# 48-column state products, V's scalings in blocks, and a plainer end, in a delta-rule + GELU kernel

## The chip, the cores and the metric

The kernel runs on one core of one Trainium2 chip. Five engines share the work: TensorE (PE in the profile; its weight loads are the row PEld), VectorE (DVE), ScalarE (ACT), GpSimd (POOL) and SyncE (SP), which here only issues DMAs. The metric is the time of one execution on the device, in microseconds. The profile is that of one execution, and its span runs from the first to the last instruction.

## The reference

Two blocks follow each other. The first is a delta rule, a linear attention whose state is corrected at each of 768 steps, for 4 x 8 heads of 48 elements. The second is a two-layer network with an exact GELU on the 3072 tokens.

```python
k_n = k / (np.linalg.norm(k, axis=-1, keepdims=True) + 1e-06)
state = zeros((B, H, D, D))                      # B=4, H=8, S=768, D=48
for t in range(S):
    y[:, :, t] = q[:, :, t] @ state              # per head
    v_old      = state^T k_t
    state      = state + beta_t * outer(k_t, v_t - v_old)
x = y.transpose(0, 2, 1, 3).reshape(3072, 384)
h = x @ w_in                                     # 384 -> 2048
g = 0.5 * h * (1.0 + erf(h / sqrt(2)))
out = g @ w_out                                  # 2048 -> 384
```

## The kernel before

The sequence is cut into 12 chunks of 64 steps (`C = 64`, `NC = 12`). A unit is one chunk of two batches, so a chunk has two units (`u.a` is 0 or 1); the two batches lie in the two halves of the 128 partitions. `D` is 48, `H` is 8, `NP` is 4 pairs of heads, `NA` is 2. The scaled differences inside a chunk are found with a triangular inverse of 32-row blocks, which VectorE computes for two chunks at a time (`eliminate`), and 32x32 products on TensorE join the blocks (`psJ`). K in memory isn't normalised: V is multiplied by K's norm instead.

The state step of a chunk is `against_state` (old values and outputs from the state), `solve`, `outputs`, and `turn`:

```python
    HALF = [slice(0, C), slice(C, 2 * C)]
    QUADS = [(0, 0), (1, 1), (0, 1), (1, 0)]

    def scale_head(u, h):
        nc.scalar.mul(u.V[:, h], u.V[:, h], ns[u.c][:, u.a, h:h + 1])

    def scale_v(u, engine=nc.gpsimd):
        engine.tensor_tensor(u.V, u.V, ns[u.c][:, u.a].unsqueeze(2).to_broadcast([128, H, D]),
                                op=ALU.mult)
    ...
    def use(us):
        for u in us:
            psY = dn("psY")
            u.psY = quarters(psY[:, :, 0:NP * D])
            u.psS = psY[:, :, NP * D:2 * NP * D].rearrange("q p (j d) -> q p j d", d=D)
            ...                                  # u.psY: 64-column products of P and U
            if u.c > 0:
                update(u)

    def update(u):
        if u.c < NC - 1:
            for j in range(NP):
                for r, p in QUADS:
                    nc.tensor.matmul(u.psS[HALF[r], p, j, :], lhsT=u.Kp[HALF[p], 2 * j + r, :],
                                     rhs=u.U[HALF[p], 2 * j + r, :], start=True, stop=True)

    def next_state(u):
        if u.c < NC - 1:
            nc.vector.tensor_tensor(St[:, u.a], St[:, u.a], u.psS, op=ALU.add)

    def read(u, copy=nc.scalar.copy):            # x = psY + y, four operations
        ...

    def outputs(us):
        use(us)
        for u in us:
            next_state(u)
            read(u)
```

A row of K holds 48 elements and 16 columns of zeros (`Kp` is 64 wide), so the product has 64 rows per head, of which 48 count. `turn` transposes x on TensorE into `xT`, and ScalarE copies it out of PSUM. The network follows. The first layer, `fc1`, makes 128 rows of h at a time for the 256 tokens of a chunk; two PSUM buffers ("mlp") alternate, and ScalarE's GELU empties them. From chunk 2 on the second layer is a 2x2 block product with 7 products in place of 8; T1 to T4 are sums and differences of the weights. Its products use the same two "mlp" buffers, plus one for Z:

```python
    def fc1(c, f):
        psH = ps.tile([128, NA * 128], F32, tag="mlp", name="psH")
        for m in range(NM):
            nc.tensor.matmul(psH, lhsT=w_in_sb[...], rhs=xTs[c][:, m, :], ...)
        nc.scalar.activation(G[:, f, :], psH, ACT.Gelu)

    def send(u, cols=slice(0, DM), queues=(nc.scalar, nc.scalar)):
        for p in range(2):
            row = (2 * u.a + p) * S + u.c * C
            queues[p].dma_start(out=out[row:row + C, cols], in_=u.o[HALF[p], cols])

    def fc2(u, f0, f1):                          # chunks 0 and 1 only
        ...                                      # psO, an "mlp" buffer, one per unit
        if f1 == NF:
            u.o = wk.tile([128, DM], F32, tag="o_sb", name="o_sb")
            nc.scalar.copy(u.o, u.psO)
            send(u)

    def sums_of_w():
        for n, a, b in ((1, B12, B11), (2, B22, 1), (4, B21, 2)):
            T[n] = more[0].tile([128, FH, DH], F32, name=f"T{n}")
            nc.vector.tensor_tensor(T[n], a, b if n == 1 else T[b], op=ALU.subtract)

    def two(c, n):                               # order of n: 1, 5, 2, 6, 4, 7, 3
        ...
        elif n == 6:
            W2["Y"] = ps.tile([128, 2, DH], F32, tag="mlp", name="psY2")
            product(W2["Y"][:, 0], A[0][0], T[2], True)
        elif n == 7:
            product(W2["Y"][:, 0], A[1][0], T[3], False)
        ...
        else:
            W2["V"] = W2["Y"][:, 1] if c < NC - 1 else dn("psV2")[:, 0, 0:DH]
            product(W2["V"], A[0][1], B22, True)

    def read2(c, n):
        if n == 6:   ...                         # u2 = Y[:, 0] + p1
        elif n == 7: ...                         # u3 = Y[:, 0] + p1; o[1] and its send; u2 = Z + u2
            nc.scalar.copy(o[0][:, 0:DH], X[:, 0])
            tiles[c, 0].o = o[0]
            if c == NC - 1:
                send(tiles[c, 0], slice(0, DH), (nc.sync, nc.sync))
        else:
            nc.vector.tensor_tensor(o[0][:, DH:], W2["V"], W2["u2"], op=ALU.add)
            if c == NC - 1:
                send(tiles[c, 0], slice(DH, DM), (nc.sync, nc.scalar))
            else:
                send(tiles[c, 0])
```

Everything after the first chunk's state is emitted by a plan: each step has a time, in units in which the network of chunk c runs from c + 1 to c + 2, and steps are emitted in order of these times. VectorE keeps this order. The instructions of the other engines are ordered when the kernel is compiled, with the emission order as their priority.

```python
    plan += [at(0.985, 1.26, decode_steps(3, n_in)), at(1.26, 1.65, decode_steps(n_in, NW)), at(1.66, 1.67, [(1.0, late)])]
    ...                  # at(1.65, 1.655, finish_both): the norms that scale V of chunks 2 and 3
    ...                  # at(2.72, 2.98, state_steps(2)), at(2.97, 2.971, finish of chunk 4)
    plan += [at(0.995, 1.0, [(1.0, load_v, 2)]), at(2.98, 2.981, [(1.0, sums_of_w)]), at(3.1, 3.11, [(1.0, last_sum_of_w)])]
    plan += [at(c - 0.4, c - 0.3, v_steps(c)) for c in range(4, NC)]
    plan += [at(2.08, 2.44, [(1.0, scale_head, tiles[c, a], h)
                             for c in (2, 3) for a in range(NA) for h in range(H)])]
    ...
        t = {4: 2.73, 5: 2.95}.get(c, c - (1.97 if c % 2 == 0 else 2.36))
        plan += [at(t, t + 0.01, [(1.0, turned_k, u) for u in us])]
    ...                  # at(w + 0.09, w + 0.092, gram + query) for odd w: at w = 3 the grams of chunk 5
    with tc.manual_schedule(engines={mybir.EngineType.DVE}):
        emit(*plan)
```

`turned_k` is a transposition of K by 32x32 blocks on VectorE, and the grams of the chunk on TensorE read its result.

Of the kernel before, what the change touches and what calls it, by code (L numbers as in the profile page):

```python
# [11 lines left out]
ALU = mybir.AluOpType  # L12
# [4 lines left out]
def kernel(  # L17
# [28 lines left out]
    nc = tc.nc  # L46
    B, H, S, D = q.shape
    DM, DF = moe_w_in.shape
    C = 64
    HB = 32  # L50
    NC = S // C
    NP = H // 2
    NA = B // 2
# [4 lines left out]
    HALF = [slice(0, C), slice(C, 2 * C)]  # L58
# [10 lines left out]
    def dn(name):  # L69
        return ps.tile([128, 2, 512], F32, tag="dn", name=name)  # L70
# [20 lines left out]
    tiles = {}  # L91
# [7 lines left out]
    for c in range(NC):  # L99
        for a in range(NA):  # L100
            u = tiles[c, a] = Unit()
# [77 lines left out]
    St = cpool.tile([128, NA, 2, NP, D], F32)  # L179
# [75 lines left out]
    Ds, Gs, Nus, XMs, gms, ns = {}, {}, {}, {}, {}, {}  # L255
# [69 lines left out]
            nc.vector.tensor_tensor(r, r, x, op=ALU.mult)  # L325
            nc.vector.scalar_tensor_tensor(x if i == 2 else s, s, 0.5, r, ALU.mult, ALU.add)

    def scale_head(u, h):
        nc.scalar.mul(u.V[:, h], u.V[:, h], ns[u.c][:, u.a, h:h + 1])

    def scale_v(u, engine=nc.gpsimd):
        engine.tensor_tensor(u.V, u.V, ns[u.c][:, u.a].unsqueeze(2).to_broadcast([128, H, D]),  # L332
                                op=ALU.mult)

# [205 lines left out]
    def v_steps(c):  # L540
        return [(1.0, scale_v, tiles[c, a]) for a in range(NA)]
# [78 lines left out]
    def update(u):  # L620
        if u.c < NC - 1:
            for j in range(NP):
                for r, p in QUADS:
                    nc.tensor.matmul(u.psS[HALF[r], p, j, :], lhsT=u.Kp[HALF[p], 2 * j + r, :],  # L624
                                     rhs=u.U[HALF[p], 2 * j + r, :], start=True, stop=True)

    def next_state(u):
        if u.c < NC - 1:
            nc.vector.tensor_tensor(St[:, u.a], St[:, u.a], u.psS, op=ALU.add)

    def read(u, copy=nc.scalar.copy):
        u.x = wk.tile([128, H, D], F32, tag="x", name="x")
# [36 lines left out]
    DH = DM // 2  # L669
    B11, B12 = w_out_sb[:, 0:FH, 0:DH], w_out_sb[:, 0:FH, DH:]  # L670
    B21, B22 = w_out_sb[:, FH:, 0:DH], w_out_sb[:, FH:, DH:]
# [6 lines left out]
                             rhs=xTs[c][:, m, :], start=(m == 0), stop=(m == NM - 1))  # L678
        nc.scalar.activation(G[:, f, :], psH, ACT.Gelu)  # L679

    def send(u, cols=slice(0, DM), queues=(nc.scalar, nc.scalar)):
        for p in range(2):
            row = (2 * u.a + p) * S + u.c * C
            queues[p].dma_start(out=out[row:row + C, cols], in_=u.o[HALF[p], cols])

    def fc2(u, f0, f1):
        if f0 == 0:
# [22 lines left out]
    A = [[G[:, k * FH:(k + 1) * FH, a * 128:(a + 1) * 128] for k in range(2)] for a in range(NA)]  # L710
    W2 = {}

    def product(ps_, lhs, rhs, first):
        for f in range(FH):
            nc.tensor.matmul(ps_, lhsT=lhs[:, f, :], rhs=rhs[:, f, :], start=first and f == 0,  # L715
                             stop=f == FH - 1, skip_group_check=not first)
# [14 lines left out]
    def two(c, n):  # L731
        if n == 1:
            W2["X"] = ps.tile([128, 2, DH], F32, tag="mlp", name="psX2")
            W2["o"] = [wk.tile([128, DM], F32, tag="o_sb", name="o_sb") for a in range(NA)]
            product(W2["X"][:, 0], A[0][0], B11, True)
        elif n == 5:
            W2["Z"] = small[0].tile([128, DH], F32, tag="z", name="psZ2")
            product(W2["Z"], W2["S"], T[1], True)
            W2["p1"] = more[0].tile([128, DH], F32, tag="p1", name="p1")
            nc.scalar.copy(W2["p1"], W2["X"][:, 0])  # L740
# [3 lines that stand above are left out]
        elif n == 2:  # L744
            product(W2["X"][:, 0], A[0][1], B21, False)
        elif n == 7:
            product(W2["Y"][:, 0], A[1][0], T[3], False)
        elif n == 4:
            product(W2["X"][:, 1], A[1][1], T[4], True)
        else:  # L750
            W2["V"] = W2["Y"][:, 1] if c < NC - 1 else dn("psV2")[:, 0, 0:DH]
            product(W2["V"], A[0][1], B22, True)

    def read2(c, n):
        o, X, Y, Z = W2["o"], W2["X"], W2["Y"], W2["Z"]
        if n == 6:
            W2["u2"] = more[0].tile([128, DH], F32, tag="u2", name="u2")
            nc.vector.tensor_tensor(W2["u2"], Y[:, 0], W2["p1"], op=ALU.add)
        elif n == 7:
            W2["u3"] = more[0].tile([128, DH], F32, tag="u3", name="u3")  # L760
            nc.vector.tensor_tensor(W2["u3"], Y[:, 0], W2["p1"], op=ALU.add)  # L761
            nc.vector.tensor_tensor(o[1][:, 0:DH], X[:, 1], W2["u3"], op=ALU.add)
            nc.vector.tensor_tensor(o[1][:, DH:], Z, W2["u3"], op=ALU.add)
            tiles[c, 1].o = o[1]
            send(tiles[c, 1])
            nc.scalar.copy(o[0][:, 0:DH], X[:, 0])
            nc.vector.tensor_tensor(W2["u2"], Z, W2["u2"], op=ALU.add)
            tiles[c, 0].o = o[0]
            if c == NC - 1:
                send(tiles[c, 0], slice(0, DH), (nc.sync, nc.sync))  # L770
        else:
            nc.vector.tensor_tensor(o[0][:, DH:], W2["V"], W2["u2"], op=ALU.add)
            if c == NC - 1:
                send(tiles[c, 0], slice(DH, DM), (nc.sync, nc.scalar))
            else:
                send(tiles[c, 0])

    def first_layer(c, f):
        fc1(c, f)
# [22 lines left out]
    def at(first, last, steps):  # L802

        total, done, timed = sum(s[0] for s in steps), 0.0, []
        for w, *step in steps:
            timed.append((first + (last - first) * (done + 0.5 * w) / total, step))
            done += w
        return timed
# [108 lines left out]
    def late():  # L917
# [3 lines left out]
        for a in range(NA):  # L921
# [3 lines left out]
            for c in range(5, NC, 2):  # L925
# [11 lines left out]
             at(2.58, 2.74, join_steps(1)), at(2.72, 2.98, state_steps(2)),  # L937
             at(2.67, 2.671, [(1.0, prep, 4)]), at(2.8, 2.9, [(1.0, grams, [tiles[4, a] for a in range(NA)])])]
    plan += [at(0.995, 1.0, [(1.0, load_v, 2)]), at(2.98, 2.981, [(1.0, sums_of_w)]), at(3.1, 3.11, [(1.0, last_sum_of_w)])]
    plan += [at(c - 0.4, c - 0.3, v_steps(c)) for c in range(4, NC)]  # L940
    plan += [at(2.08, 2.44, [(1.0, scale_head, tiles[c, a], h)
                             for c in (2, 3) for a in range(NA) for h in range(H)])]
    plan += [at(c - 1.0, c - 0.99, [(1.0, load_v, c)]) for c in range(3, NC)]
    for c in range(4, NC):
        us = [tiles[c, a] for a in range(NA)]
        t = {4: 1.8, 5: 2.1}.get(c, c - 2.9)
        plan += [at(t, t + 0.01, [(1.0, load_blocks, c, "Kb", k)])]
        t = 3.2 if c == 4 else c - (1.3 if c % 2 == 0 else 0.9)
        plan += [at(t, t + 0.01, [(1.0, load_blocks, c, "Qb", q)])]
        t = c - (2.1 if c % 2 == 0 else 2.6) if c > 5 else {4: 2.1, 5: 2.69}[c]  # L950
        plan += [at(t, t + 0.01, [(1.0, load_k, c, "Kn")])]
        plan += [at(c - 0.4, c - 0.39, [(1.0, load_k, c, "Kp")])]
        t = {4: 2.73, 5: 2.95}.get(c, c - (1.97 if c % 2 == 0 else 2.36))
        plan += [at(t, t + 0.01, [(1.0, turned_k, u) for u in us])]
        t = c + (0.05 if c % 2 == 0 else -0.34)
        plan += [at(t, t + 0.01, [(1.0, turned_q, u) for u in us])]
# [56 lines left out]
```

## Time and profile before

| | |
|---|---|
| time, median of 3 | 671.63 us (670.9 to 671.82) |
| span of the profiled execution | 670.1 us |
| mean granted TensorE clock | 0.969 |
| TensorE busy in 120-141 / 141-160 / 160-178.5 / 186-206 us | 20.99 of 21.0 / 17.79 of 19.0 / 17.59 of 18.5 / 20.0 of 20.0 |
| VectorE busy in 186-206 / 206-230 us | 18.39 of 20.0 / 21.62 of 24.0 |
| state products (psY L624) | 704 matmul instructions, 218 ns each at the median |
| state additions (St L629) | 22 operations, 554 ns at the median |
| V's scalings on ScalarE (V L329) | 32 operations, 325 ns at the median, first at 118.5, last at 130.5 us |

An fp32 product shows as two matmul instructions and two weight loads. The 218 ns of a matmul is the time from its start to the end of its result; [...] instructions follow each other far more closely than that. A line of the timeline gives the start, the duration, the engine, the line of the code, the operation, what it writes and reads, and the number of instructions merged; in brackets stands how long its engine had been idle, and for what. A product into a tile that shares memory with `psY` is shown under that name, so the state products appear as psY at line 624. The chain of waits is followed back from the last instruction: at each step to what released it.

### The profile page before, as it was taken

To read this page: it belongs to the slowest core of one execution; us is meant where nothing else is said; L and a number is where in the kernel's file an instruction comes from. 1 tells how busy PE (TensorE), PEld (TensorE's weight loads), DVE (VectorE), ACT (ScalarE), POOL (GpSimd) and SP (SyncE) were. 2 spreads that over 40 slices of the span, in tenths; PEclk is the share of its full clock that TensorE was granted. 3 is DMA by queue.
4 is the path that set the end of the run, shared out by engine and by line. 5 is a ranking of instruction groups with operands and counts; after the bars stand their busy time and mean duration, and the time that the engine had idled before them with its cause. 6 is when DMAs were issued, how large, how long until landed. Compare 5 with 4: busy or idle time off the path is not lost.

```text
span 670.1 us, 21705 instructions
## 1 busy us (share of the span) xinstructions
PE 640.3 (96%) x9542; PEld 559.4 (83%) x9542; DVE 452.3 (67%) x921; ACT 228.6 (34%) x605; POOL 82.1 (12%) x82
## 2 busy tenths in 40 slices
PE   5767998999999999999999999999999999999997
PEld 4656775866689989989989989989989989989997
DVE  6999999994689846489846479846479844324021
ACT  3357754714342143142143142143142133122220
POOL 4051300103111021111021111021111010000000
PEclk8576999999999999999999999999999999999999
DMA  9785655203431232511332511211401210100101
GB/s 130 174 253 167 121 172 135 48 0 66 81 51 32 53 53 44 82 31 30 55 49 49 84 29 26 53 21 30 68 3 24 55 20 3 24 2 2 24 1 25
DMA packets 158431, 39.76 MB, mean 59 GB/s; under 512 B 150016, under 2 KB 153216, under 8 KB 158336
## 3 DMA queue, kind: packets, MB, share of 16 engines
q1 hardware_dynamic: 152464, 33.40, 26.3%
q10 hardware_dynamic: 5872, 4.97, 3.2%
q8 instruction: 75, 1.23, 0.8%
q14 instruction: 20, 0.16, 0.1%
HBM read 33.62 MB, written 4.72 MB: 57 GB/s over the span
## 4 chain that ended last, share of the span: by engine, by line
PE 82%; DVE 10%; ACT 3%; issue 2%; DMA 2%; SPq 1%; DVEq 0%; ACTq 0%
PE psH L677 36%; PE psX L715 12%; PE psY L715 12%; PE psZ L715 4%; PE psJ L517 3%; PE psK L572 3%; PE psG L367 3%; PE psO L690 2%; PE psU L597 2%; DVE Nu L444 2%; DVE tmp L442 2%; PE psY L615 1%; DVE w_e L235 1%; DVE w_out_sb L236 1%; PE psY L624 1%
## 5 line engine op out<-in xcount | busy, mean ns | idle before, releaser
L677 PE MATMUL psH<-xT,w_in_sb 128*128 128x256 f32 x1152 | 261.5, 383 | 2.3 <-ACT G L679 2.3
L677 PEld LDWEIGHTS psH<-xT,w_in_sb 128*128 128x128 f32 x1152 | 215.6, 190 | 33.7 <-ACT G L679 3.9
L679 ACT ACTIVATE G<-psH 128x256 f32<-128x256 f32 x192 | 73.3, 382 | 180.4 <-PE psH L677 168.3
L444 DVE TENSOR_TENSOR Nu<-Nu,tmp 128x30 f32<-128x30 f32 (+9 forms) x180 | 61.8, 343 | 6.2
L442 DVE TENSOR_TENSOR tmp<-Nu 128x30 f32<-128x30 f32 (+9 forms) x180 | 61.6, 342 | 5.1
L715 PE MATMUL psX<-w_out_sb,G 128*128 128x192 f32 x320 | 56.2, 329 | 0.0
L715 PE MATMUL psY<-w_out_sb,G 128*128 128x192 f32 x304 | 54.1, 329 | 0.6
L715 PEld LDWEIGHTS psX<-w_out_sb,G 128*128 128x128 f32 x320 | 52.2, 190 | 0.7
L715 PEld LDWEIGHTS psY<-w_out_sb,G 128*128 128x128 f32 x304 | 49.1, 190 | 2.1 <-DVE u L761 1.8
L690 PE MATMUL psO<-w_out_sb,G 128*128 128x384 f32 x128 | 45.1, 495 | 1.6 <-DVE w_out_sb L236 1.6
L660 ACT COPY xT<-psX 128x384 f32<-128x384 f32 x24 | 11.3, 476 | 102.9 <-PE psX L659 102.8
L306 POOL TENSOR_TENSOR n<-n,half 128x16 f32<-128x16 f32 x10 | 29.4, 2938 | 87.9 <-DVE n L281 66.9
L690 PEld LDWEIGHTS psO<-w_out_sb,G 128*128 128x128 f32 x128 | 23.1, 190 | 16.9 <-DVE w_out_sb L236 4.0
L603 ACT COPY U<-psU 64x192 f32<-64x192 f32 x96 | 30.0, 313 | 19.5 <-PE psU L597 18.3
L402 DVE TENSOR_TENSOR P<-psG,mask 128x1024 f32<-128x1024 f32 x10 | 12.2, 1224 | 35.6 <-PE psG L367 35.6
L580 DVE TENSOR_TENSOR W<-psK,V 128x384 f32<-128x384 f32 x22 | 12.1, 552 | 29.1 <-ACT y L579 29.0
L466 POOL MEMSET Zf<- 32x512 f32 x23 | 12.4, 541 | 154.5 <-DVE Zf L457 153.6
L724 DVE TENSOR_TENSOR S<-G 128x512 f32<-128x512 f32 x20 | 13.7, 687 | 25.8 <-ACT G L679 25.7
L332 POOL TENSOR_TENSOR V<-V,n 128x384 f32<-128x384 f32 x18 | 17.1, 958 | 106.1 <-DMA V<-in_v_dram 67.6
L638 DVE TENSOR_TENSOR x<-psY,y 64x192 f32<-64x192 f32 x80 | 28.3, 354 | 0.9
L715 PE MATMUL psY<-T,G 128*128 128x192 f32 x160 | 28.2, 329 | 0.0
L715 PE MATMUL psX<-T,G 128*128 128x192 f32 x160 | 28.1, 329 | 0.0
(138 smaller groups left out, 866.9 us busy)
## 6 DMA issues: line engine op xcount, KB each, us to landing
Kp<-in_k_dram SPq DMA_DIRECT2D x76, 96.0 KB, 3.6
w_out_sb<-in_moe_w_in_dram SPq DMA_DIRECT2D x24, 256.0 KB, 4.2
V<-in_v_dram SPq DMA_DIRECT2D x48, 96.0 KB, 2.9
out_dram<-o_sb ACTq DMA_DIRECT2D x46, 96.0 KB, 2.2
w_raw<-in_moe_w_out_dram SPq DMA_DIRECT2D x10, 384.0 KB, 5.4
Zf<-in_moe_w_out_dram SPq DMA_DIRECT2D x6, 384.0 KB, 5.1
Qp<-in_q_dram SPq DMA_DIRECT2D x64, 32.0 KB, 2.2
Qp<-in_q_dram SPq DMA_DIRECT2D x16, 96.0 KB, 4.3
```

Of the source, the lines that this page charges most:

```text
L306: nc.gpsimd.tensor_tensor(flat, flat, half, op=ALU.pow)
L367: nc.tensor.matmul(psG[HALF[p], r, i * NP + j, :], lhsT=u.Kt[rows, p, j, :], rhs=(u.Qt if x else u.Kt)[rows, p, j, :], start=True, stop=True)
L442: nc.vector.tensor_tensor(tmp, nu[:, j + 1:, j:j + 1].to_broadcast([128, n, j]), nu[:, j:j + 1, 0:j].to_broadcast([128, n, j]), op=ALU.mult)
L444: nc.vector.tensor_tensor(nu[:, j + 1:, 0:j], nu[:, j + 1:, 0:j], tmp, op=ALU.add)
L517: nc.tensor.matmul(psJ[to, i, :], lhsT=(xm if level else off)[rows, u, :], rhs=zf[rows, u, HB:C] if level else xm[rows, u, :], start=True, ...
L572: nc.tensor.matmul(u.psK[to, x, r, j, :], lhsT=(u.Qt if x else u.Kt)[rows, p, j, :], rhs=St[rows, u.a, p, j, :], start=True, stop=True)
L603: copy(pairs(u.U[HALF[p]], s), u.psU[HALF[p ^ s], p])
L638: nc.vector.tensor_tensor(dst, src, pairs(u.y[HALF[p ^ s]], s), op=ALU.add)
L677: nc.tensor.matmul(psH, lhsT=w_in_sb[:, f // 2, m, f % 2 * 128:(f % 2 + 1) * 128], rhs=xTs[c][:, m, :], start=(m == 0), stop=(m == NM - 1))
L679: nc.scalar.activation(G[:, f, :], psH, ACT.Gelu)
L690: nc.tensor.matmul(u.psO, lhsT=G[:, f, u.a * 128:(u.a + 1) * 128], rhs=w_out_sb[:, f, :], start=(f == 0), stop=(f == NF - 1))
L715: nc.tensor.matmul(ps_, lhsT=lhs[:, f, :], rhs=rhs[:, f, :], start=first and f == 0, stop=f == FH - 1, skip_group_check=not first)
```

## The change

The headline is the product of the state: for chunks 2 and later the stationary operand is cut to K's 48 real columns, so that 48 rows per head are written and 16 columns of zeros are no longer loaded. The rows between are then not written, and the state is added in two operations, one for each range of 48 partitions. Chunks 0 and 1 keep 64 columns.

The diff carries more than that. The scalings of V for chunks 2 and 3, still 8 operations per unit on ScalarE, are emitted in blocks at 1.66 to 1.7 and at 2.6 to 2.7 in place of one by one between 2.08 and 2.44. K of chunk 5 is turned at 2.98, behind the sums of the weights, in place of 2.95. And the end loses its special treatment: the last product goes into the second half of Y as in the other chunks, and the last unit's output is sent whole, by ScalarE's queue alone.

```diff
-    def scale_head(u, h):
-        nc.scalar.mul(u.V[:, h], u.V[:, h], ns[u.c][:, u.a, h:h + 1])
-
     def scale_v(u, engine=nc.gpsimd):
+        if u.c in (2, 3):
+            for h in range(H):
+                nc.scalar.mul(u.V[:, h], u.V[:, h], ns[u.c][:, u.a, h:h + 1])
+            return
         engine.tensor_tensor(u.V, ...)
@@ update
-                    nc.tensor.matmul(u.psS[HALF[r], p, j, :], lhsT=u.Kp[HALF[p], 2 * j + r, :],
+                    m = C if u.c < 2 else D
+                    nc.tensor.matmul(u.psS[r * C:r * C + m, p, j, :],
+                                     lhsT=u.Kp[HALF[p], 2 * j + r, 0:m],
                                      rhs=u.U[HALF[p], 2 * j + r, :], start=True, stop=True)
@@ next_state
-            nc.vector.tensor_tensor(St[:, u.a], St[:, u.a], u.psS, op=ALU.add)
+            for rows in [slice(0, 128)] if u.c < 2 else [slice(r * C, r * C + D) for r in range(2)]:
+                nc.vector.tensor_tensor(St[rows, u.a], St[rows, u.a], u.psS[rows], op=ALU.add)
@@ send
-    def send(u, cols=slice(0, DM), queues=(nc.scalar, nc.scalar)):
+    def send(u):
...
-            queues[p].dma_start(out=out[row:row + C, cols], in_=u.o[HALF[p], cols])
+            nc.scalar.dma_start(out=out[row:row + C, :], in_=u.o[HALF[p]])
@@ two, the last product
-            W2["V"] = W2["Y"][:, 1] if c < NC - 1 else dn("psV2")[:, 0, 0:DH]
-            product(W2["V"], A[0][1], B22, True)
+            product(W2["Y"][:, 1], A[0][1], B22, True)
@@ read2
-            if c == NC - 1:
-                send(tiles[c, 0], slice(0, DH), (nc.sync, nc.sync))
-        else:
-            nc.vector.tensor_tensor(o[0][:, DH:], W2["V"], W2["u2"], op=ALU.add)
-            if c == NC - 1:
-                send(tiles[c, 0], slice(DH, DM), (nc.sync, nc.scalar))
-            else:
-                send(tiles[c, 0])
+        else:
+            nc.vector.tensor_tensor(o[0][:, DH:], Y[:, 1], W2["u2"], op=ALU.add)
+            tiles[c, 0].o = o[0]
+            send(tiles[c, 0])
@@ the plan
-    plan += [at(c - 0.4, c - 0.3, v_steps(c)) for c in range(4, NC)]
-    plan += [at(2.08, 2.44, [(1.0, scale_head, tiles[c, a], h)
-                             for c in (2, 3) for a in range(NA) for h in range(H)])]
+    plan += [at(max(c - 0.4, 1.66), c - 0.3, v_steps(c)) for c in range(2, NC)]
@@
-        t = {4: 2.73, 5: 2.95}.get(c, c - (1.97 if c % 2 == 0 else 2.36))
+        t = {4: 2.73, 5: 2.98}.get(c, c - (1.97 if c % 2 == 0 else 2.36))
```

## The prediction, made before the changed kernel was run

> **What bounds the kernel now.** I read the page from the top: shares of busy time, the slices, then the chain that ended last.
>
> ```profile
> PE 640.3 (96%) x9542; PEld 559.4 (83%) x9542; DVE 452.3 (67%) x921; ACT 228.6 (34%) x605; POOL 82.1 (12%) x82
> PE   5767998999999999999999999999999999999997
> PEclk8576999999999999999999999999999999999999
> PE 82%; DVE 10%; ACT 3%; issue 2%; DMA 2%; SPq 1%; DVEq 0%; ACTq 0%
> ```
>
> TensorE is the bound: from the seventh slice on it is full at nearly full clock, and 82% of the chain is matmuls. A part of the change counts if it takes TensorE instructions away, makes them shorter, or makes TensorE wait. So I looked at the places the diff touches for what TensorE waits on there. First the timeline where V of chunks 2 and 3 is scaled (start, duration, engine, line):
>
> ```profile
> 117.38 2.85 PE L690 MATMUL psO<-w_out_sb,G 128*128 128x384 f32 x8 [0.47 <-DVE w_out_sb L236]
> 118.46 0.55 ACT L329 ACTIVATE V<-V,n 128x48 f32<-128x48 f32 x2
> 118.97 0.48 ACT L694 COPY o_sb<-psO 128x384 f32<-128x384 f32 x1
> 120.06 4.11 PE L677 MATMUL psH<-xT,w_in_sb 128*128 128x256 f32 x17
> 127.29 1.22 ACT L329 ACTIVATE V<-V,n 128x48 f32<-128x48 f32 x5
> ```
>
> The copy at 118.97 frees the PSUM buffer that the first layer of chunk 1 starts in at 120.06. The scalings around it fill gaps. Next the state step of chunk 2 and its end, then that of chunk 3:
>
> ```profile
> 172.36 0.55 DVE L629 TENSOR_TENSOR St<-St,psY 128x384 f32<-128x384 f32 x1 [7.61 <-PE psY L624]
> 174.79 1.46 DVE L638 TENSOR_TENSOR x<-psY,y 64x192 f32<-64x192 f32 x4
> 176.49 0.53 ACT L278 ACTIVATE ksq<-Kp 128x384 f32<-128x384 f32 x1 [5.64 <-DVE x L638]
> 178.55 4.15 PE L677 MATMUL psH<-xT,w_in_sb 128*128 128x256 f32 x18
> ...
> 221.29 0.36 DVE L758 TENSOR_TENSOR u<-psY,p 128x192 f32<-128x192 f32 x1
> 221.81 2.77 PE L715 MATMUL psY<-w_out_sb,G 128*128 128x192 f32 x16
> ```
>
> In chunk 2 the chain runs through VectorE's x into ScalarE, xT and the first layer. In chunk 3, VectorE's u ends only 0.16 us before the product that accumulates onto the psY it reads. Last, the end, and the weight loads by number of columns:
>
> ```profile
> 664.03 2.61 PE psV L715 x16
> 666.67 0.36 DVE o_sb L772
> ...
> L624 PEld LDWEIGHTS psY<-U,Kp x704: 135/135/228, 58.1 to 572.4; 64*64 64x64 f32 x176
> L517 PEld LDWEIGHTS psJ<-XM,G x640: 101/108/108, 146.3 to 544.9; 32*32 32x32 f32 x160
> ```
>
> [...] 108, 135 and 190 ns for 32, 64 and 128 columns, 0.84 to 0.86 ns per column above a fixed part. [...] the state products of one unit follow the previous group after 0.47 us for 32 instructions, 14.7 ns each, although one load lasts 135. [...] The trace has 325, and five in 1.22 us are spaced by (1.22 - 0.325)/4 = 0.224 us.
>
> **Part 1, 48 columns.** Chunks 2 to 10 have 9 x 2 units x 16 products x 2 passes = 576 instructions. At 64 columns the pace is 14.7 ns. The 32-column products of the joins, where two sets alternate over four tiles, run 128 in (1.26 - 0.19) us, 8.4 ns each. Their moving operand is shorter too, but psG with 64 moving columns keeps the pace of psY with 48 (in the chain 120 of them take 1.91 us and 64 take 1.09, 14.6 ns for each one more), so I take the stationary columns as the limit. Half way: 11.5 ns, 3.1 less. 576 x 3.1 ns = **-1.8 us**, 0.2 per chunk.
>
> **Part 2, the state added in two parts.** One VectorE operation more per unit; an addition is followed 0.47 us later by the next operation, so x of the second unit comes 0.95 us later. VectorE has 33% idle, so this costs only where TensorE waits. Even chunks from 4: x ends at 376.03 in chunk 6, its transposition starts at 378.24; no cost. Chunk 2: whole on the chain, +1.0. Chunk 3: u would end at 222.60 against 221.81; with the 0.2 that part 1 had brought forward, +1.0. Chunks 5, 7, 9: in chunk 5, u ends at 321.66 and the product starts at 322.71; the slack of 1.0 nearly holds it, but TensorE arrives 0.2 earlier: +0.15 each. Sum **+2.5 us**. The two parts of the headline together thus cost about 0.7.
>
> **Part 3, V's scalings.** Only VectorE follows the plan by hand; the other engines' order is set at compile time, with ready work of the earlier plan time first, and idle gaps filled (the scalings planned for 2.08 to 2.44 all ran by 130.9 us). Now chunk 2's sixteen stand at 1.67 to 1.69, ahead of the o_sb copies near 2.0. They become ready when VectorE has n, at 117.4, behind two fills of Kb. So I expect sixteen in a row from 118.5: 15 x 0.224 + 0.325 = 3.7 us, where two, 0.55 us less overlap, stood before the copy. The copy moves from 118.97 to about 122.1, and everything behind it in ScalarE's order by the same 3.1: the first layer waits for its buffer at 120.22, gets it after 122.6, and then pays again for the second copy and the first GELU, which queue behind output issues of 1.19 us. TensorE is 3.1 us late. From there to 173 us it idles little; the gap of 0.59 at 150.5 in the chain, where it waits for VectorE, absorbs its size. **+2.5 us**. Chunk 3's sixteen still fill GELU gaps.
>
> **Part 4, K of chunk 5 turned behind the weight sums.** Two transpositions, 1.30 us together, change places with three sums, 5.3 us. VectorE's work is unchanged. But the grams of chunk 5, begun at 177.91 and resumed at 183.07, can start only near 185.5, and masks and elimination follow them. TensorE can fill with first-layer products; VectorE may idle, and chunk 3 has no VectorE slack (busy 21.6 of 24 us from 206 to 230), so idle time reaches the 0.16 us slack above. I put **+0.8**, between nothing and 2.
>
> **Part 5, the end.** The last product goes back into the bank of the sum that VectorE reads first. Beside chunk 5's state step this wait is seen: products end at 325.60, the next ones at 328.90, 3.30 us for 2.61, so +0.7. Both output parts then go from one queue, the second issue about 0.55 later; but the last 48 KB pieces from the other queue took 3.0 us to land, ScalarE's 96 KB pieces 2.2. 0.7 + 0.55 - 0.8 = about **+0.5**.
>
> Sum: -1.8 + 2.5 + 2.5 + 0.8 + 0.5 = +4.5, so 671.6 + 4.5 = 676.1 us, 0.7% slower.
>
> **Rivals.** (a) The compile-time order keeps the copies ahead of the sixteen scalings, as now. Then part 3 is nought, 673.6. For it: the order now puts the copy behind just two. Against it: those two have the later plan time and still went first because they were ready. (b) The load of 48 columns costs as much as 64, by strips of 32 or because instructions, not columns, set the pace: 677.9. For it: moving sizes of 48 and 64 don't differ. Against it: 8.4 ns at 32. (c) Every wait is hidden, because TensorE's order is made anew for the later VectorE results, and only the shorter products and the end remain: 671.6 - 1.8 + 0.5 = 670.3. For it: TensorE has first-layer products to put in. Against it: x of chunk 2 and u of chunk 3 come where the order has nothing left. (d) VectorE idles for chunk 5's grams, and the lateness runs through the elimination into chunks 3 and 4: 3 more, 679.
>
> **Range and chances.** Every part is below 0.5%; together the costs reach 8 to 9 us at worst. 2% is 13.4 us, which no sum of them reaches; a gain is capped at 1.8 plus what a new order finds. Range 672.3 to 679.5, from (c) and (a) half way to (d). Within 2%: 0.95.
>
> **What will show it.** Loads of the state products at some 121 ns, and 32 of them in about 0.37 us instead of 0.47: part 1. In chunk 2, x later by a microsecond and the first layer with it; in chunk 3 TensorE waiting for u: part 2. An unbroken run of sixteen scalings near 118 us and a hole in TensorE near 120: part 3. VectorE idle before the masks near 186 us: part 4. TensorE waiting for u in the last chunk: part 5. A time under 672 would say that waits I call exposed are hidden; over 680, that the compile-time order of TensorE has got worse in a way no part accounts for.

## The result: 1.1% slower, and the profile after

| | before | after |
|---|---|---|
| time, median (lowest to highest) | 671.26 us (670.63 to 671.82) | 678.5 us (677.76 to 679.25) |
| ratio, 95% interval | | 1.0108 (1.009 to 1.0126) |
| span of the profiled execution | 670.1 us | 676.1 us |
| mean granted TensorE clock | 0.969 | 0.985 |

The change costs 7.2 us (671.26 x 0.0108; interval 6.0 to 8.5). The prediction was 676.1 us with a range of 672.3 to 679.5: the direction and the range hold, and the loss is about 1.6 times the 4.5 us that the sum of the parts gave. The page of the changed kernel, busy time, slices and shares of the chain:

```profile
PE 641.3 (95%) x9542; PEld 557.9 (83%) x9542; DVE 463.7 (69%) x939; ACT 228.9 (34%) x605; POOL 82.7 (12%) x82
PE   6858998899799999999999999999999999999997
PEclk9976999999999999999999999999999999999999
PE 73%; DVE 19%; ACT 3%; issue 3%; DMA 1%; POOL 0%; ACTq 0%; SPq 0%; DVEq 0%; POOLq 0%
```

TensorE has as many instructions as before and is busy one microsecond longer; its share of the chain falls from 82 to 73%, and VectorE's rises from 10 to 19%. So the loss is waiting: 18 additions more put VectorE on the chain in places where it had been just behind it. VectorE is still only 69% busy, so that share alone would not have shown it.

To find the places I took the start of the same TensorE instruction in both traces at the border of each stretch. A positive step is time that the changed kernel loses there.

| stretch, times of the kernel before | shift at its end, us | step, us | what the prediction had for it, us |
|---|---|---|---|
| up to 118 us | -0.5 | -0.5 | none |
| the wait for the psO buffer, near 120 | +2.0 | +2.5 | hole of 3.1 |
| on to the readouts of chunk 2 at 158.4 | +0.5 | -1.6 | 0.6 of it absorbed |
| to the first layer of chunk 2 at 178.6 | +1.0 | +0.5 | +1.0 - 0.2 |
| to the readouts of chunk 3 at 196.4 | +2.8 | +1.8 | +0.8 |
| chunk 3, to 254.7 | +4.0 | +1.3 | +1.0 - 0.2 |
| chunks 4, 6, 8, 10 together | | -0.4 | 4 x -0.2 |
| chunks 5, 7, 9, each | | +0.33 | +0.15 - 0.2 |
| from chunk 11 to the last product | +5.2 | +0.6 | +0.7 |
| from the last product to the end of the span | +6.0 | +0.8 | -0.2 |

The two profiled executions took 671.82 and 677.84 us, so they are 6.0 us apart and the medians 7.2. The profiled one of the kernel before was long: its span is 670.1 us, and its 26 executions beside the first four experiments have spans of 668.4 to 670.9 with a median of 669.1. Part of that, 0.8 us, lies in chunk 2 (see end_one_queue), so a step there is read against a wait that not every execution has.

**The hole near 120 us.** Timeline of the changed kernel (start, duration, engine, line; in brackets the idle time and its releaser):

```profile
117.97 3.70 ACT L331 ACTIVATE V<-V,n 128x48 f32<-128x48 f32 x16
121.57 0.83 ACT L698 COPY o_sb<-psO 128x384 f32<-128x384 f32 x2
122.08 13.15 PE L681 MATMUL psH<-xT,w_in_sb 128*128 128x256 f32 x58 [2.35 <-ACT o_sb L698]
124.60 0.76 ACT L683 ACTIVATE G<-psH 128x256 f32<-128x256 f32 x2 [2.19 <-DMA out_dram<-o_sb]
```

Sixteen scalings run in one row of 3.70 us, the copy that frees the psO buffer starts at 121.57 instead of 118.97, and TensorE stands still for 2.35 us. The second loss that I had expected here, at the first GELU, is not there: TensorE runs 58 instructions in a row.

**Chunk 2.** The same view between 172 and 180 us:

```profile
172.61 1.12 DVE L633 TENSOR_TENSOR St<-St,psY 48x384 f32<-48x384 f32 x2 [8.34 <-PE psY L626]
176.14 0.52 ACT L278 ACTIVATE ksq<-Kp 128x384 f32<-128x384 f32 x1 [4.93 <-DVE x L642]
176.36 1.46 DVE L642 TENSOR_TENSOR x<-psY,y 64x192 f32<-64x192 f32 x4
178.99 0.48 ACT L664 COPY xT<-psX 128x384 f32<-128x384 f32 x1 [1.38 <-PE psX L663]
179.52 2.86 PE L681 MATMUL psH<-xT,w_in_sb 128*128 128x256 f32 x12 [1.03 <-ACT xT L664]
```

x of the second unit ends at 177.82 instead of 176.25, 1.57 us later, but the first layer starts only 0.97 later. Before, ksq ran at 176.49, held up the copy of xT behind it, and so had the first layer wait as well; the prediction saw x alone there. end_one_queue below shows what ksq waited for.

**Grams of chunk 5, then chunk 3.** Two views of the changed kernel, 182 to 192 us, and u in chunk 3:

```profile
184.98 1.30 DVE L353 STREAM_TRANSPOSE Kt<-Kb 128x512 f32<-128x512 f32 x2
185.74 0.56 PE L368 MATMUL psG<-Kt 48*64 48x64 f32 x20 [1.63 <-DVE Kt L353]
188.72 1.23 DVE L403 TENSOR_TENSOR P<-psG,mask 128x1024 f32<-128x1024 f32 x1 [1.68 <-PE psG L368]
...
225.32 0.36 DVE L761 TENSOR_TENSOR u<-psY,p 128x192 f32<-128x192 f32 x1
225.74 2.54 PE L719 MATMUL psY<-w_out_sb,G 128*128 128x192 f32 x14 [1.23 <-DVE u L761]
```

TensorE does not fill the time with first-layer products, as I had thought: it stands for 1.63 us until the first half of K of chunk 5 is turned, and then VectorE stands for 1.68 us until the grams are there (0.52 before). In chunk 3, u was 0.16 us early; now TensorE waits 1.23 us for it.

**Chunk 5, and the loads of the state products.** Timeline, and the group of the loads (min/median/max ns, first and last start, forms):

```profile
319.70 0.54 PE L626 MATMUL psY<-U,Kp 64*48 64x48 f32 x32
320.06 0.65 PE L616 MATMUL psY<-U,P 64*64 64x48 f32 x32
321.41 1.11 DVE L633 TENSOR_TENSOR St<-St,psY 48x384 f32<-48x384 f32 x2
322.54 1.46 DVE L642 TENSOR_TENSOR x<-psY,y 64x192 f32<-64x192 f32 x4
327.07 2.87 PE L719 MATMUL psY<-w_out_sb,G 128*128 128x192 f32 x16 [0.28 <-DVE u L761]
...
L626 PEld LDWEIGHTS psY<-U,Kp x704: 122/122/228, 57.6 to 577.0; 64*48 64x48 f32 x144, 64*64 64x64 f32 x32
```

A load of 48 columns takes 122 ns, and the group of 32 is followed after 320.06 - 319.70 = 0.36 us, both as predicted. The additions are not: from the first to x there are 322.54 - 321.41 = 1.13 us, where one addition took 0.47. That is 0.66 more per unit, 1.3 per chunk, and not 0.47 and 0.95.

**The end:**

```profile
669.08 2.87 PE L719 MATMUL psY<-w_out_sb,G 128*128 128x192 f32 x16 [0.45 <-DVE u L764]
669.71 3.84 ACTq L688 DMA_DIRECT2D out_dram<-o_sb  x4
671.98 0.36 DVE L772 TENSOR_TENSOR o_sb<-psY,u 128x192 f32<-128x192 f32 x1 [2.04 <-PE psY L719]
```

The last product writes the second half of Y, whose first half u is read from, and waits 0.45 us for u. In plain_end, in Y as well, it starts 3.05 us after the product ahead of it (661.16 and 664.21 in the chain); in end_one_queue, in a bank of its own, 2.60 after it (659.71 and 662.31). From the end of the last addition (672.34) to the end of the span are 3.76 us; before they were 3.07 (667.03 to 670.1).

### The profile page after: what moved, and what is told of

Its sections match the earlier page's. It is cut to its first block, busy times and chain, and to the rows that moved or that the text cites. A ratio compares the mean times of both kernels' runs of the same rounds, so it can differ in the third digit from the quotient of the medians.

```text
span 676.1 us, 21722 instructions
## 1 busy us (share of the span) xinstructions
PE 641.3 (95%) x9542; PEld 557.9 (83%) x9542; DVE 463.7 (69%) x939; ACT 228.9 (34%) x605; POOL 82.7 (12%) x82
## 3 DMA queue, kind: packets, MB, share of 16 engines
q8 instruction: 75, 1.23, 0.8%
## 4 chain that ended last, share of the span: by engine, by line
PE 73%; DVE 19%; ACT 3%; issue 3%; DMA 1%; POOL 0%; ACTq 0%; SPq 0%; DVEq 0%; POOLq 0%
PE psH L681 32%; PE psY L719 11%; PE psX L719 10%; PE psZ L719 3%; DVE Nu L445 3%; DVE tmp L443 3%; PE psJ L518 3%; PE psK L573 3%; PE psG L368 3%; PE psO L694 3%; DVE x L642 2%; PE psU L598 2%; DVE St L633 1%; DVE w_e L235 1%; DVE w_out_sb L236 1%
## 5 line engine op out<-in xcount | busy, mean ns | idle before, releaser
L719 PE MATMUL psY<-w_out_sb,G 128*128 128x192 f32 x320 | 57.4, 331 | 3.1 <-DVE u L761 2.1
L719 PEld LDWEIGHTS psY<-w_out_sb,G 128*128 128x128 f32 x320 | 51.6, 190 | 5.8 <-DVE u L761 3.0
L664 ACT COPY xT<-psX 128x384 f32<-128x384 f32 x24 | 11.3, 476 | 103.4 <-PE psX L663 103.3
L633 DVE TENSOR_TENSOR St<-St,psY 48x384 f32<-48x384 f32 (+1 forms) x40 | 21.9, 551 | 11.2 <-PE psY L626 10.6
L526 DVE TENSOR_TENSOR XM<-psJ,gm 32x512 f32<-32x512 f32 x20 | 13.8, 690 | 22.0 <-PE psJ L518 21.8
```

The costliest lines, as they stand in the source:

```text
L633: nc.vector.tensor_tensor(St[rows, u.a], St[rows, u.a], u.psS[rows], op=ALU.add)
```

## The experiments

Each ratio is against the kernel before, run beside it (median 670.8 to 670.9 us). "Shift" is the same comparison of TensorE's starting times as in the table above.

### The four parts, each alone

**headline**: only the two edits that the change is named for.

```diff
-  nc.tensor.matmul(u.psS[HALF[r], p, j, :], lhsT=u.Kp[HALF[p], 2 * j + r, :], ...)
+  m = C if u.c < 2 else D
+  nc.tensor.matmul(u.psS[r * C:r * C + m, p, j, :], lhsT=u.Kp[HALF[p], 2 * j + r, 0:m], ...)
-  nc.vector.tensor_tensor(St[:, u.a], St[:, u.a], u.psS, op=ALU.add)
+  for rows in [slice(0, 128)] if u.c < 2 else [slice(r * C, r * C + D) for r in range(2)]:
+      nc.vector.tensor_tensor(St[rows, u.a], St[rows, u.a], u.psS[rows], op=ALU.add)
```

> The kernel before with the 48-column products and the state added in two parts, and nothing else of the change. In the trace of the changed kernel the second addition moves the end of x by 1.3 us per chunk, not by the 0.95 of the prediction, and TensorE waits for u in the odd chunks. Theory A (the additions cost more than the shorter loads bring): chunk 2 +0.4, chunk 3 +1.2, chunks 5, 7 and 9 +0.33 each, even chunks 0 to -0.2: together +1.5 to +2.5 us. Rival B (the shorter loads win, and chunk 3 was late only because K was turned behind the weight sums): -1 to 0 us.

Measured: 674.0 us (673.65 to 675.22), ratio 1.0052 (1.004 to 1.0064), so +3.5 us, the largest of the four. The shift grows by 0.8 us up to the first layer of chunk 2, by 1.4 in chunk 3 and by 0.33 in each of chunks 5, 7 and 9; chunks 8 and 10 gain 0.2 each, chunks 4 and 6 nothing. The headline is a loss by itself, and larger than the 0.7 us of the prediction.

**v_blocks**: only the scalings of V.

```diff
-  plan += [at(c - 0.4, c - 0.3, v_steps(c)) for c in range(4, NC)]
-  plan += [at(2.08, 2.44, [(1.0, scale_head, tiles[c, a], h) for c in (2, 3) ...])]
+  plan += [at(max(c - 0.4, 1.66), c - 0.3, v_steps(c)) for c in range(2, NC)]
   # and scale_v scales chunks 2 and 3 head by head on ScalarE, as in the change
```

> The kernel before with V's scalings in blocks of sixteen, and nothing else. Both theories expect the hole of 2.4 us in TensorE near 120 us. Theory A (TensorE had idle stretches between 150 and 158 us, where it waited for the join blocks, and the hole takes their place): the delay at the state step of chunk 2 is some 1.0 us and stays so to the end: +0.7 to +1.3 us. Rival B (the prediction's: nearly all of it stays): +2.3 to +3 us.

Measured: 673.12 us (672.52 to 673.41), ratio 1.0033 (1.0022 to 1.0045), +2.2 us, between the two theories. The shift at the hole is +2.5 us against the start of the program, as in the changed kernel, and of what has gathered by 146 us 1.75 us are absorbed by 158 us, again as there. But another 1.5 us are lost between the two places. The windows over 117 to 141 us (TensorE's busy time and instructions, loads, VectorE, ScalarE, GpSimd, granted clock, DMA share, GB/s), first v_blocks, then the changed kernel:

```profile
117.00:141.00 24.00, 21.65 (x89) 17.73 (x88) 21.85 (x59) 13.35 (x49) 1.92 (x1) 0.93 0.21 34
```

```profile
117.00:141.00 24.00, 21.55 (x94) 17.60 (x95) 21.91 (x58) 13.83 (x50) 1.91 (x1) 1.00 0.21 34
```

With the same hole the granted clock is 0.93 in the first and 1.00 in the second, and TensorE is busy 21.65 / 89 = 0.243 us for each instruction in the first and 21.55 / 94 = 0.229 in the second. From the clocks alone I estimate the loss at 0.07 x 24 = 1.7 us, about the 1.5. So in this trace the hole costs 0.8 us net, and by this estimate the clock took nearly twice as much on top. That the hole caused the dip is not shown: the same hole is there in the changed kernel without it. The times leave a part open too. All six executions lie within 0.9 us, at least 1.6 above the median of the kernel before; only one of them was profiled, so either the dip came in most of them or something else adds to the 0.8.

**v_behind_copies**: chunk 2's sixteen scalings still in one block, but placed in the plan behind the copies of the output.

```diff
-  plan += [at(2.08, 2.44, [(1.0, scale_head, tiles[c, a], h) for c in (2, 3) ...])]
+  plan += [at(2.03, 2.031, [(1.0, scale_head, tiles[2, a], h) ...])]
+  plan += [at(2.6, 2.7, [(1.0, scale_head, tiles[3, a], h) ...])]
```

> The kernel before with chunk 2's scalings emitted as a block at 2.03, just behind the copies of the second layer's output and just ahead of the first GELUs of chunk 1: twelve in a row now stand in front of the first GELU. Theory A (a block of ScalarE's work costs what TensorE waits for behind it, copy or GELU): the hole moves from the first product of chunk 1 to its third, 2 to 2.5 us of it, and +0.7 to +2.5 us in the end. Rival B (only the copies matter, the GELUs have two buffers to hide behind): no hole, -0.3 to +0.3 us.

Measured: 671.31 us (670.58 to 671.85), ratio 1.0007 (0.9998 to 1.0015): no difference that this interval shows. Timeline:

```profile
122.83 2.80 ACT L329 ACTIVATE V<-V,n 128x48 f32<-128x48 f32 x12
125.95 10.41 PE L677 MATMUL psH<-xT,w_in_sb 128*128 128x256 f32 x47 [1.40 <-ACT G L679]
```

Twelve scalings run in a row all the same, now ahead of a GELU, and TensorE waits 1.40 us for it. The shift is +1.8 us at 146 us and 0.0 at 158 us. So a hole in TensorE here costs nothing up to some 1.75 us: that is what the stretch from 146 to 158 us absorbs, in all three traces. In the chain of the kernel before there are two gaps in it, 0.59 us at 150.46 and 0.62 at 154.18; both are gone from the chains of the three. They are 1.2 of the 1.75; where the rest comes from is not shown.

**k_behind**: only K of chunk 5.

```diff
-  t = {4: 2.73, 5: 2.95}.get(c, ...)
+  t = {4: 2.73, 5: 2.98}.get(c, ...)
```

> The kernel before with K of chunk 5 turned behind the weight sums, and nothing else. Theory A (TensorE's order is fixed with the grams of chunk 5 in front of first-layer products, and it stands idle until K is turned): TensorE idle 1.5 to 2 us near 185 us for the turned K, total +1.5 to +2 us. Rival B (the prediction's: TensorE fills, and VectorE's late elimination costs in chunk 3): no idle near 185, TensorE waits for u near 221 instead, +0.8 us or less.

Measured: 672.06 us (671.41 to 674.54), ratio 1.0021 (1.0012 to 1.003), +1.4 us. TensorE waits 0.62 us for K, the shift grows by 0.7 from the first layer of chunk 2 to the readouts of chunk 3, and chunk 3 adds 0.5 by u: half the one theory, half the other. In the changed kernel the first of these stretches cost 1.8 us. There the sums and transpositions of VectorE follow an x that ended 2.5 us later than in k_behind (177.82 against 175.35). The turning of K starts as much later (184.98 against 182.50), but the first layer only 1.9 (179.52 against 177.61), which makes up 0.6 of the 1.0 us by which TensorE's wait is longer there. By these traces the two edits make each other worse; a run with these two alone was not tried.

**plain_end** and **end_one_queue**: the end of the change; and the end with ScalarE's queue alone for whole pieces, but the last product in a bank of its own as before.

```diff
-  W2["V"] = W2["Y"][:, 1] if c < NC - 1 else dn("psV2")[:, 0, 0:DH]
+  W2["V"] = W2["Y"][:, 1]                     # plain_end only
-  send(tiles[c, 0], slice(0, DH), (nc.sync, nc.sync))
-  send(tiles[c, 0], slice(DH, DM), (nc.sync, nc.scalar))
+  send(tiles[c, 0])                           # both
```

> The kernel before with the plain end, and nothing else. Theory A: the last product starts 0.7 us later because VectorE reads the bank first, and the two whole output pieces from one queue land 0.7 us later than the halves from two queues: +1.2 to +1.6 us. Rival B (the prediction's: ScalarE's pieces land 0.8 us sooner after their issue than the other queue's, so the second issue costs nothing): +0.4 to +0.7 us.

> The kernel before with whole output pieces from ScalarE's queue alone at the end; the last product keeps a bank of its own. Of the 1.1 us of the plain end this leaves out the wait for the bank. Theory A (bank 0.7 us, queue 0.7 us, as the trace of plain_end has them: 3.8 us from the last output sum to the end, 3.1 before): +0.4 to +0.8 us. Rival B (the bank's wait is the whole): 0 to +0.2 us.

Measured: plain_end 672.07 us (671.41 to 672.99), ratio 1.0017 (1.0009 to 1.0025), +1.1 us; its last product starts 0.6 us later, and from the last addition to the end there are 3.8 us. end_one_queue 670.92 us (670.57 to 672.3), ratio 1.0004 (0.9995 to 1.0012), no difference that this interval shows, though in its trace the tail is 3.8 us long too (665.31 to 669.1). So by the times most of the 1.1 us is the bank, and by the traces the queue costs 0.7 in the tail; the interval, -0.3 to +0.8 us, holds both none and 0.7, so the queue's share stays open. The trace of end_one_queue had gained elsewhere, in chunk 2, which it does not touch:

```profile
172.84 0.52 ACT L278 ACTIVATE ksq<-Kp 128x384 f32<-128x384 f32 x1 [2.98 <-issue]
173.94 0.48 ACT L660 COPY xT<-psX 128x384 f32<-128x384 f32 x1 [0.57 <-PE psX L659]
176.79 4.15 PE L677 MATMUL psH<-xT,w_in_sb 128*128 128x256 f32 x18
```

In the kernel before, ksq ran at 176.49, and the copy of xT behind it in ScalarE's order at 176.92, although its psX had been ready since 174.9. Here ksq runs at 172.84, and the first layer starts 1.53 us after the end of x (175.26) and not 2.30. ksq reads a K that is being loaded, and the traces hold when each load lands. The first piece of Kp in that stretch was issued at 172.27 in the kernel before and landed at 176.42, 0.07 us ahead of ksq; here it was issued at 170.25 and landed at 172.77, again 0.07 us ahead; in the changed kernel it landed at 176.06, ksq ran at 176.14. So the wait ahead of ksq, which the profile puts down to VectorE's x, was for this transfer, and it cost the profiled execution of the kernel before 0.8 us. The piece took 4.0 to 4.2 us to land in the traces of before, k_behind and v_behind_copies, and 2.5 to 2.8 in those of end_one_queue, plain_end, two_adds and cols_late. No run edits this load, so it differs from one execution to the next, and the gain is not the edit's. An edit that takes the wait away was not tried.

### What the second addition costs, and whether it can be moved

**two_adds**: 64 columns as before, two additions. **half_add**: 48 columns, but from chunk 2 on only rows 0 to 47 are added; it leaves the state of the other half of the heads as it was. **mixed**: 48 columns for one half of the heads and 64 for the other, so that one addition of 112 rows is enough.

```diff
   # two_adds: next_state of the change alone; half_add and mixed: one addition of
+  rows = slice(0, 128) if u.c < 2 else slice(0, D)          # half_add
+  rows = slice(0, 128) if u.c < 2 else slice(0, C + D)      # mixed
+  m = C if u.c < 2 or r == 0 else D                         # mixed
```

> The kernel before with the state added in two operations of 48 rows; the products keep 64 columns. This is the cost of the second addition alone. In the headline run it made TensorE late by 0.3 us in each odd chunk, by 1.4 us in chunk 3 and by some 0.6 us in chunk 2. Theory A (the second addition is the whole cost, and the shorter loads bring something in the even chunks only): 0.4 to 0.8 us slower than the headline run, +3 to +4 us against before. Rival B (the 48-row outputs themselves disturb TensorE or PSUM): this run costs less than half of the headline run.

> The kernel before with 48-column products and one addition, of the first 48 rows only; the other half of the heads' state is left out after chunk 2. So VectorE has as many operations as before, and the shorter loads stand alone. Theory A (0.2 us per chunk, on the path everywhere once no addition is in the way): -1.2 to -1.8 us. Rival B (waits of chunks 2 and 3 swallow it): -0.6 us or less.

> The kernel before with 64 columns for the first head of a pair and 48 for the second, so that rows 0 to 111 are all written and one addition of 112 rows suffices. In a round of four products each half of the rows loads one operand of 64 and one of 48 columns. Theory A (loads of one row half follow each other, so a round takes the sum of two loads): half of the gain of 48 columns, 32 products in 0.42 us, -0.6 to -0.9 us. Rival B (each of the four tiles has its own pace, and the 64-column tile sets the round): 0.47 us for 32, no gain, -0.2 to +0.3 us.

Measured: two_adds 674.93 us (673.99 to 675.4), ratio 1.006 (1.0048 to 1.0073), +4.0. half_add 669.16 (668.61 to 670.28), ratio 0.9978 (0.997 to 0.9987), -1.5, in the shift 0.1 us in chunk 3 and 0.2 in each chunk from 4 to 10. mixed 670.87 (670.34 to 671.87), ratio 1.0002 (0.9993 to 1.001).

So the shorter products are worth 1.5 us (0.9 to 2.0), where part 1 said 1.8, and the second addition takes away about 5 (from -1.5 to +3.5); with 64 columns, in two_adds, it costs 4.0. In chunk 2 an addition of 48 rows in half_add is followed after 0.47 us (171.60, x at 172.07), one of 112 rows in mixed after 0.47 (172.40, 172.87), one of 128 before after 0.47 (172.36, 172.83): half the rows save nothing. And mixed gains nothing: half its state products load 48 columns, but a group of 32 is still followed after 0.47 us, and the four groups of chunk 5 take 2.01 us (314.85 to 316.86) as before (315.17 to 317.18), against 1.80 in half_add (313.54 to 315.34). So in these rounds of four products the widest load set the pace.

**cols_late**: headline, with both additions of a chunk moved behind x of both units, and in odd chunks behind the first u. **cols_later**: in odd chunks further, behind the second u and all output sums but the last. **cols_grouped**: as cols_later, but rows 0 to 47 of both units first, then rows 64 to 111 of both.

```diff
   for u in us:
-      next_state(u)
+      if u.c < 2:
+          next_state(u)
       read(u)
+  t = 2.972 if w == 2 else w + 0.8 if w % 2 else w + 0.86   # cols_late; w + 0.905 in the other two
+  plan += [at(t, t + 0.0002, [(1.0, next_state, tiles[w, a]) for a in range(NA)])]
+  # cols_grouped: ... (next_state, tiles[w, a], r) for r in range(2) for a in range(NA)
```

> The kernel before with 48-column products and the state added in two parts, but behind x of both units and behind u, where nothing waits for it until the next chunk. Theory A (the additions cost only by their place): x comes 1 us earlier than before, the loads' gain of 1.8 us is kept, chunk 2 gains another 0.5 to 1 us: -1.5 to -3 us. Rival B (VectorE is full in the odd chunks, and the additions delay the elimination or W instead): -0.5 us or slower.

> As cols_late, but in the odd chunks the additions stand behind the second u and the output sums too; in cols_late they stood ahead of the second u, and TensorE waited for it in chunk 3 (2.0 us later there). Theory A (the additions cost by their place only): chunk 3 loses nothing, every chunk from 2 to 10 gains 0.2, chunk 2 up to 0.5 more: -1.5 to -2.5 us. Rival B (VectorE is simply too full in chunk 3, and wherever the additions stand something waits): chunk 3 again 1 us or more late, total -0.5 to +1 us.

> As cols_later, but the four additions of a chunk are ordered by rows: rows 0 to 47 of both units, then rows 64 to 111 of both. In the traces an addition of rows 0 to 47 is followed 0.46 us later by an operation that starts at partition 0, and 0.56 us later by one that starts at partition 64. Theory A (an operation overlaps its predecessor by 0.1 us only if both start at the same partition): starts of the four spaced 0.46, 0.56, 0.46. Rival B (two additions to the state never overlap, because of what they read and write): 0.56 three times. Time within 0.5 us of cols_later.

Measured: cols_late 673.43 us (672.07 to 674.31), ratio 1.0039 (1.0026 to 1.0052). cols_later 673.25 (672.13 to 675.01), 1.0038 (1.0024 to 1.0053). cols_grouped 672.59 (671.88 to 673.37), 1.0025 (1.0015 to 1.0035). All are better than headline at the median (1.0052), clear of its interval (from 1.004) only cols_grouped; none gets back to the kernel before. In cols_late the shift does not grow in chunk 2, but its trace lacks the 0.8 us that the kernel before waits for ksq's transfer, which may hide a loss. Chunk 3 has a new wait, the second u behind the additions:

```profile
222.62 2.24 DVE L632 TENSOR_TENSOR St<-St,psY 48x384 f32<-48x384 f32 x4
227.40 2.87 PE L719 MATMUL psY<-w_out_sb,G 128*128 128x192 f32 x16 [2.09 <-DVE u L765]
```

In cols_later that wait is gone, chunk 3 costs 0.8 us instead of 2.05, the even chunks gain their 0.2 each in full, and the odd ones lose 0.53. In chunk 5 the shift jumps by 0.7 us at one place, where the first layer waits 0.47 us for its own first GELU. The timeline shows the four additions, the last output sum and the place, first in cols_later; of cols_grouped the additions alone:

```profile
327.14 2.24 DVE L632 TENSOR_TENSOR St<-St,psY 48x384 f32<-48x384 f32 x4
330.56 0.36 DVE L776 TENSOR_TENSOR o_sb<-psY,u 128x192 f32<-128x192 f32 x1
330.99 3.29 PE L681 MATMUL psH<-xT,w_in_sb 128*128 128x256 f32 x14 [0.47 <-ACT G L683]
```

```profile
327.15 2.05 DVE L632 TENSOR_TENSOR St<-St,psY 48x384 f32<-48x384 f32 x4
```

The last output sum reads the second half of Y, and so frees one of the two "mlp" buffers. Before, it ran at 328.94 and the second psH of the chunk, at 330.03, waited by its semaphore for VectorE, that is, for Y's buffer. Here the sum stands behind the additions and four steps of the elimination, and the second psH waits for the GELU of the first psH instead, that is, for the other buffer. So work moved off u has landed on the next hand-over; additions behind this last sum were not tried.

In cols_grouped the work is the same, and the order alone saves VectorE 0.19 us. In rows 0, 64, 0, 64 each follows the one ahead by (2.24 - 0.55) / 3 = 0.56 us, so none overlaps its neighbour. In rows 0, 0, 64, 64 two of the three neighbours start at the same row; 2.05 - 0.55 = 1.50 fits 0.47 + 0.56 + 0.47.

## Why the prediction was right, and where it fell short

**Part 1, 48 columns: right.** 11.3 ns for each instruction against 11.5, loads of 122 ns, 0.2 us per chunk, -1.5 us in half_add for the -1.8; rival (b) falls with it.

**Part 2, the second addition: the term that failed.** Together with part 1 it was to cost 0.7 us; headline measured 3.5. The places were right (x in chunk 2, u in chunk 3, u in chunks 5, 7 and 9), the size per unit was not. I took 0.47 us, the spacing of an addition and x as they stood; that 48 rows take as long as 128 was an estimate of mine, which the later traces bear out (0.55 us in both). That spacing includes an overlap of 0.1 us, which a second part loses twice: 0.56 to the other part and 0.57 to x. In these traces the overlap goes with the row at which the parts start: rows 64 to 111 behind rows 0 to 47 have none, nor has x, which starts at row 0 again, behind rows 64 to 111. cols_grouped agrees: by order alone its four additions take 2.05 us in place of 2.24. What in VectorE makes the difference is not shown. So x of the second unit comes 1.3 us later and not 0.95. The slack of 1.0 us in chunks 5, 7 and 9 does not hold that: +0.33 each, where I had -0.05. (By the product's own start, 322.81, that slack is 1.15.) Chunk 3 paid 1.3 for 0.8. Chunk 2 alone paid less in the changed kernel, 0.5 for 0.8: in the trace that the prediction read, the first layer was waiting for ksq as well, so x was not the whole chain. In executions where that transfer lands in time the same delay of x should cost some 0.8 more, an estimate from the 2.30 and 1.53 us under end_one_queue. And "no cost" in the even chunks held for 8 and 10 only. In chunk 6 the later x pushes VectorE's n (381.62 in the changed kernel, 376.04 before) and through it two ksq on ScalarE (382.25, 376.68); the copy of xT stands behind these (383.14, with its psX ready at 382.87), the next weight load waits 0.28 us for it, and in headline the 0.2 of part 1 is gone. cols_late, where x comes earlier, keeps it.

**Part 3, the block of scalings: right in kind, and in sum by luck.** +2.5 predicted, +2.2 measured alone. Its terms were off in three ways: a hole of 2.5 us and not 3.1, since nothing was paid a second time at the GELU; 1.75 us of it absorbed and not 0.59, as I had counted one gap of two and other time is absorbed besides; and a dip of the clock in the trace of v_blocks, which I had not thought of and which makes up for the two. In the changed kernel, without the dip, the net is some 0.8. Rival (a), copies ahead of the block, falls: the sixteen scalings start at 117.97 in the changed kernel and the copy at 121.57, in the order of the plan. v_behind_copies shows that the place ahead of the copies was the mistake, not the block: its wait of 1.4 us stays under what is absorbed.

**Part 4, K of chunk 5: right in sign, half the size.** +0.8 predicted, +1.4 alone, +1.8 in the changed kernel. "TensorE can fill with first-layer products" is what failed: it waited 0.62 us alone, and 1.63 behind the later x. Rival (d) had VectorE's idle time right (1.68 us), but of the 3 us that it saw run on, k_behind shows 0.5 in chunk 3 and none in chunk 4.

**Part 5, the end: bank right, transfers wrong.** The bank's 0.7 us was measured as 0.6. The second issue costs what I said: it starts at 672.9, 0.6 us behind the last addition, where both pieces went at 667.1, 0.1 behind it. But the 0.8 us that I credited to ScalarE's faster landing did not come: the tail is 0.7 us longer in all three traces with one queue.

**The sum.** 3.5 + 2.2 + 1.4 + 1.1 = 8.2 us for the four parts alone, against 7.2 (6.0 to 8.5) together; the differences are within the intervals, and the clock's dip is in the trace of one of them. The 4.5 of the prediction lies below this mostly by part 2, which was 2.8 short. Rival (c), all waits hidden, falls with headline, where TensorE waits at every place that part 2 names.

## What to carry to other kernels

Before an operation is split, count it at its full price, and look at where the parts start: on VectorE two parts that start at rows 0 and 64 cost 1.13 us where one of 128 rows was followed after 0.47, and of the 0.66 us lost per unit the shorter matmuls gave back 0.11. A bound of 96% TensorE does not make the other engines free: what counts is the slack at each hand-over, here 0.16 us in one chunk and 1.0 in others, and work moved off one hand-over can land on the next, as in chunk 5 of cols_later (0.47 us for the first GELU). When the profile names as releaser an engine that was done long ago, look for a transfer before putting that wait on a chain: here K landed 0.07 us ahead of ksq. And before a trace serves as the base of a comparison, set its span beside those of other executions: here the base stood 1.0 us above their median.

## What the runs showed of the hardware

- In a round of four state products the widest load set the pace: a group of 32 instructions was followed after 0.47 us with 64 columns (before), 0.36 with 48 (the changed kernel), 0.47 with half of each (mixed).
- A VectorE addition of 384 fp32 elements from PSUM took 0.54 to 0.56 us with 48 rows (the changed kernel) and with 128 (before), 0.56 with 112 (mixed). The next operation started 0.46 to 0.48 us after it where it began at the same row (before, half_add, mixed, k_behind, plain_end), and 0.55 to 0.57 where it didn't (the changed kernel).
- With the same hole of 2.4 us in TensorE the granted clock over the 24 us around it was 0.93 in one trace (v_blocks) and 1.00 in another (the changed kernel); what decides is open.
- The same 96 KB load, which no run edits, took 2.5 us to land in one execution (end_one_queue) and 4.2 in another (before). In the second, ksq on ScalarE started at 176.49, 0.07 us behind its landing, and the copy of xT behind ksq at 176.92, although its psX had been ready since 174.9.
